# A state-space layer beside a feed-forward layer: the first tile's statistics, two weight pieces and a reciprocal block are reordered

## The chip, the cores and the metric

The kernel runs on one core of a Trainium2 chip. A core has a matrix engine (TensorE, in the profile PE, its weight loads PEld), a vector engine (VectorE, DVE), a scalar engine (ScalarE, ACT), GpSimd (POOL), and SyncE (SP), which here only issues transfers. Each engine runs its own list of instructions in order and waits on semaphores for the others. Transfers (DMA) are issued from the queues of SyncE, ScalarE and POOL. The metric is the time of one execution on the device, in microseconds.

## The reference: what is computed

The input `u` has 2048 rows of 576. A layer norm of it goes into two branches, and input and branches are added:

```python
x = A_u
xn = _layernorm(x, axis=-1)
return x + _A_ref(xn, A_A_re, ..., A_Dskip) + _B_ref(xn, B_w1, B_w2)
```

Branch B is a feed-forward layer, `silu(xn @ w1) @ w2` with 4608 hidden columns. Branch A is a state-space convolution: from nine small parameter arrays a kernel `K` of 2048 taps is made for each of the 576 channels, and each channel of `xn` is convolved with its `K` by a Fourier transform; `xn * Dskip` is added.

## The kernel before

**Matrix products in parts.** Every operand of a large product is split in a high part, rounded to the matrix engine's short format, and a low part, the rest. A product is then three: high by high, high by low, low by high. A name that ends in `h` is a high part, one that ends in `l` a low part: `xh`, `xl` of the normed input, `w1h`, `w1l` of the first weights, `w2h`, `w2l` of the second, `gh`, `gl` of the hidden values. A high part is a copy with rounding, on ScalarE; a low part is a subtraction, on VectorE.

**Tiles and blocks.** The 2048 rows are 16 tiles of 128 rows, loaded in pairs (`load_x`, lines 167 to 177; the first pair in eight transfers over the queues of SyncE and ScalarE). Four tiles make a block of 512 rows. `phase0` (line 210) treats tiles 0 to 7 at the start: `norm` (line 185) takes the statistics on VectorE (lines 192 and 193), adds a constant (196), has POOL raise the variance to the power -0.5 (197) and scales the tile (201, or 206 on ScalarE). `put_xt` (line 120) transposes a tile on TensorE into PSUM (124) and makes `xh` (125) and `xl` (126); `put_x4` (line 128) does the same with the last 64 columns of two tiles (132 to 134). `late` (line 897) treats tiles 8 to 15, whose transposed form goes through memory.

**The feed-forward part** (`ffn`, line 256) is the main program. The hidden columns come in nine chunks of four groups of 128, and all of it runs for two halves of the rows. For each half, chunk and block, `up` (line 316) makes a hidden group: twelve matmuls over the high and low parts and two for the last 64 columns (326 to 328), then SiLU and the split of the result (334 to 337). `down` (line 339) multiplies a tile's hidden values with the second weights (352) and adds the sum to an accumulator (356). The weights are loaded by `load_w1` (263) and `load_w2` (297) and split by `split_w1` (282) and `split_w2` (305). The first block's `up` works on its first two tiles, then on the other two, so that it can begin early.

**The state-space part** (`side`, line 858) is a second program beside it. It is a generator that stops at marks, fractions of the main program's length; `weave` (line 33) runs the main program step by step and lets the other go on when its mark is reached. `natural` (line 465) prepares the parameters on VectorE and ScalarE in five pieces; between its pieces lie the marks of the list in line 906. `gate_of(i)` (line 854) gives the marks that lie at the first step of a block.

**What sets the order.** The order in which the program states instructions is a priority, not the order of execution. A planner puts each engine's instructions in order before the run, by estimated times and these priorities; on the chip each engine then keeps that order. `behind(ins)` (line 141) forces what is stated inside it behind one instruction on that instruction's own engine. `pins` holds such instructions by name: `sdv` the addition of line 196, `xn` the scaling, `pt` the last transpose, `xt_h` the high part, `xt_v` the low part of the last 64 columns, `w1l` and `w2l` the weights' low parts. `idle(n)` (line 872) issues `n` matmuls of a zero tile that nothing reads; it is called with 12 at the very start, with 8 behind tile 0's transposes and with 3 behind tile 1's.

A transfer of the first weights comes in four pieces: rows 0 to 255, rows 256 to 511, and two of 64 KB for the last 64 rows, written to the two halves of the partitions.

Of the kernel before, what the change touches and what calls it, by code (L numbers as in the profile page):

```python
# [11 lines left out]
F32 = mybir.dt.float32  # L12
# [3 lines left out]
ALU = mybir.AluOpType  # L16
# [3 lines left out]
P = 128  # L20
L = 2048
D = 576
# [4 lines left out]
HD = D // 2  # L27
# [16 lines left out]
def kernel(  # L44
# [74 lines left out]

    def put_xt(xh, xl, src):  # L120

        pt = pss.tile([P, NKT, P], F32, tag="pss", name="pt")
        for kt in range(NKT):
            pins["pt"] = nc.tensor.transpose(pt[:, kt, :], src[:, kt * P:(kt + 1) * P], ident).ins
        pins["xt_h"] = nc.scalar.copy(xh, pt).ins  # L125
        nc.vector.tensor_sub(xl, pt, xh)  # L126

    def put_x4(x4, srcs):

        pt = pss.tile([P, 512], F32, tag="pss", name="pt4")  # L130
        for i, src in enumerate(srcs):
            pins["pt"] = nc.tensor.transpose(pt[:64, i * P:(i + 1) * P], src[:, NKT * P:D], ident).ins
        pins["xt_s"] = nc.scalar.copy(x4[:64, :], pt[:64, :2 * P]).ins
        pins["xt_v"] = nc.vector.tensor_sub(x4[64:, :], pt[:64, :2 * P], x4[:64, :]).ins

    xts = {}
    pairs = {}
    lasts = []
    pins = {}

# [38 lines left out]
    def store(t, j, engines):  # L179

        for hs in (slice(0, HD), slice(HD, D)) if j == NJ - 1 else (slice(0, D),):
            for ps, v, eng in quarters(ov, engines):
                eng.dma_start(v[:, j:j + 2] if len(t.shape) > 2 else v[:, j, hs], t[ps] if len(t.shape) > 2 else t[ps, hs])

    def norm(p0, js, xs):

# [23 lines left out]
    def phase0(p0, js, idle=None):  # L210

        xs = load_x(js[0], accp, "acc", (nc.sync, nc.scalar) if js[0] < 2 else (nc.sync,))
        acc.update(zip(js, xs))
        yield
        if js[0]:
            with behind(pins["w1l"] if js[0] == 2 else None):
                normed(p0, js, xs)
        else:
            for j, xj in zip(js, xs):
                with behind(pins["xn"] if j else None):  # L220
                    normed(p0, (j,), (xj,))
                if not j:
                    pins["xt0s"] = pins["xt_h"]
                with behind(pins["pt"]):
                    idle(3 if j else 8)
        pins[f"xt{js[1]}h"] = pins["xt_h"]
        pins[f"xt{js[1]}"], pins[f"xt{js[1]}s"] = pins["xt_v"], pins["xt_s"]
        yield

    def normed(p0, js, xs):  # L230
        xn = norm(p0, js, xs)
        for i, j in enumerate(js):
            b, jj = divmod(j, 4)
            if b < 2:
                if jj == 0:
                    xts[b] = new_xt(b)
                c = slice(jj * P, (jj + 1) * P)
                xh, xl, x4 = xts[b]
                put_xt(xh[:, :, c], xl[:, :, c], xn[:, i, :])
                lasts.append(xn[:, i, :])  # L240
                if jj % 2:
                    put_x4(x4[:, (jj - 1) * P:(jj + 1) * P], lasts)
                    lasts.clear()
# [12 lines left out]
    def ffn():  # L256
# [6 lines left out]
        def load_w1(half, c, t):  # L263
# [12 lines left out]
            else:  # L276
                nc.sync.dma_start(r1[:, 0:4, :], v1)
            nc.sync.dma_start(r1[0:64, 4, :], w1[512:576, fs])
            pins["load"] = eng.dma_start(r1[64:128, 4, :], w1[512:576, fs]).ins
# [59 lines left out]
        def down(blk, jj):  # L339
# [6 lines left out]
            for h in range(2):  # L346
# [8 lines left out]
                with tc.high_priority():  # L355
                    nc.vector.tensor_add(acc[j][:, hs], po[:, :HD], acc[j][:, hs])  # L356
            if half == 0 and c == NCH - 1:
# [107 lines left out]
    def natural(nat, par):  # L465
# [54 lines left out]
        v.tensor_scalar(t0, br, 1e-37, None, op0=ALU.max)  # L520
        for i in range(0, NT, 2):
            v.reciprocal(t0[:, i:i + 2], t0[:, i:i + 2])
        v.tensor_mul(t0, t0, bi)
# [9 lines left out]
        for i in range(0, 4 * D, D):  # L533
# [324 lines left out]
    def side():  # L858
# [3 lines left out]
        with tc.tile_pool(name="kf", bufs=1) as kfp:  # L862
            for n in ("f", "phi"):
                kf[n] = kfp.tile([P, D], F32, name=n + "T")
            with tc.tile_pool(name="par", bufs=1) as par:
                with tc.tile_pool(name="pa", bufs=4) as pa:
# [28 lines left out]
                with tc.tile_pool(name="nat", bufs=1) as nat, tc.tile_pool(name="pb", bufs=1) as pb:  # L895
                    nt = natural(nat, par)
                    def late(j):
# [3 lines left out]
                        with behind(pins["xn" if j == 8 else "gl"]):  # L901
                            normed(pb, (j, j + 1), xs)
                        yield

                    tiles = chain.from_iterable(late(j) for j in range(8, NJ, 2))
                    for at, todo in ((0.0, nt), (0.0, tiles), (0.004, tiles), (0.005, tiles), (gate_of(0), nt), (0.026, tiles), (0.028, tiles), (0.036, tiles), (0.038, tiles), (gate_of(1), nt), (0.06, tiles), (gate_of(2), nt), (0.09, nt)):
# [111 lines left out]
```

## Time and profile before

| | us |
|---|---|
| median of 3 runs | 1111.88 (1111.85 to 1111.98) |
| the profiled execution | 1111.65 |
| its span, first to last instruction | 1109.9 |
| TensorE busy | 1101.6 (99%) |
| VectorE busy | 916.1 (83%) |
| ScalarE busy | 707.3 (64%) |
| POOL busy | 71.0 (6%) |
| TensorE's last matmul ends | 1105.8 |
| granted TensorE clock, mean | 1.00 |

A row of a timeline has the start, the length, the engine, the line of the kernel, the operation, what it writes and reads (`out<-in`), the shapes and how many instructions were merged; in brackets stands how long the engine was idle before it and what released it. An engine's name with a `q` is its sequencer, which issues transfers. A row of waits has who waited for whom, the total in us, how often, and the longest. A row of transfers has how many, KB each and the median us from issue to landing. Lengths of matmuls overlap, since they are pipelined.

### The profile page before, as it was taken

How to read it: one execution, taken by the hardware profiler on the slowest of the kernel's cores; microseconds unless marked ns; L12 is line 12 of the kernel's file. 1: busy time of each engine (PE TensorE's matmuls, PEld its weight loads, DVE VectorE, ACT ScalarE, POOL GpSimd, SP SyncE). 2: the span in 40 equal slices, each digit the busy share in tenths (PEclk: the TensorE clock that was granted, in tenths of full speed). 3: DMA queues.
4: the chain of work that ended last, by engine and by line, in shares of the span. 5: the costliest groups of instructions: out<-in, count | busy, mean ns of one | idle time of the engine just before them, and what ended most of it. 6: DMA issues, size and time to landing. Idle time of an engine off the chain costs nothing.

```text
span 1109.9 us, 22912 instructions
## 1 busy us (share of the span) xinstructions
PE 1101.6 (99%) x9167; PEld 997.5 (90%) x9167; DVE 916.1 (83%) x1542; ACT 707.3 (64%) x1223; POOL 71.0 (6%) x127
## 2 busy tenths in 40 slices
PE   8999999999999999999999999999999999999998
PEld 6988999899889899899989989999999999999887
DVE  7799899999999999999999837787778778784433
ACT  4574466676677676677866536877777778774210
POOL 1100000000000000011000000000000000000111
PEclk9999999999999999999999999999999999999999
DMA  8745522425242525255734163554544445434973
GB/s 255 205 123 154 146 61 61 120 72 126 77 109 82 130 62 130 77 154 163 209 127 105 44 177 105 168 159 126 160 145 150 139 147 170 130 107 130 257 205 87
DMA packets 175851, 148.56 MB, mean 134 GB/s; under 512 B 111088, under 2 KB 142720, under 8 KB 175616
## 3 DMA queue, kind: packets, MB, share of 16 engines
q1 hardware_dynamic: 165408, 112.69, 37.8%
q0 software_dynamic: 9504, 33.49, 9.5%
q8 instruction: 72, 1.18, 0.5%
q10 hardware_dynamic: 832, 0.92, 0.3%
q14 instruction: 35, 0.29, 0.1%
HBM read 102.53 MB, written 44.61 MB: 133 GB/s over the span
## 4 chain that ended last, share of the span: by engine, by line
PE 97%; DMA 2%; SPq 0%; DVE 0%; ACT 0%; issue 0%; ACTq 0%
PE po L352 42%; PE ph L326 35%; PE kp L691 3%; PE ph L327 3%; PE ph L328 3%; PE pu L821 2%; PE pb L821 2%; PE pk L821 2%; PE z L706 2%; PE pu L160 1%; PE py L842 1%; PE pu L161 1%; DMA acc<-in_A_u_dram 1%; DMA w2r<-in_B_w_dram 1%; DMA w1r<-in_B_w_dram 0%; PE ptk L485 0%
## 5 line engine op out<-in xcount | busy, mean ns | idle before, releaser
L352 PE MATMUL po<-w2l,gh 128*128 128x288 f32 x1152 | 338.6, 296 | 1.2 <-DVE w2l L313 1.2
L352 PE MATMUL po<-w2h,gl 128*128 128x288 f32 x1152 | 336.6, 295 | 0.0
L352 PE MATMUL po<-w2h,gh 128*128 128x288 f32 x1152 | 336.4, 296 | 0.0
L352 PEld LDWEIGHTS po<-w2h,gh 128*128 128x128 f32 x1152 | 215.3, 188 | 7.6 <-issue 2.8
L352 PEld LDWEIGHTS po<-w2l,gh 128*128 128x128 f32 x1152 | 216.0, 188 | 6.5 <-DVE w2l L313 1.4
L352 PEld LDWEIGHTS po<-w2h,gl 128*128 128x128 f32 x1152 | 215.6, 188 | 0.9
L334 ACT ACTIVATE gf<-ph 128x512 f32<-128x512 f32 (+1 forms) x148 | 86.3, 584 | 145.3 <-PE ph L328 133.0
L326 PE MATMUL ph<-xh,w1h 128*128 128x512 f32 (+1 forms) x592 | 161.6, 387 | 0.3 <-ACT xh L125 0.3
L326 PE MATMUL ph<-xl,w1h 128*128 128x512 f32 (+1 forms) x592 | 161.5, 386 | 0.0
L326 PE MATMUL ph<-xh,w1l 128*128 128x512 f32 (+1 forms) x592 | 161.2, 385 | 0.0
L356 DVE TENSOR_TENSOR acc<-po,acc 128x288 f32<-128x288 f32 x288 | 126.9, 454 | 36.9 <-PE po L352 35.6
L337 DVE TENSOR_TENSOR gl<-gf,gh 128x512 fp32r<-128x512 f32 (+1 forms) x148 | 99.4, 675 | 64.5 <-ACT gh L335 63.7
L326 PEld LDWEIGHTS ph<-xh,w1l 128*128 128x128 f32 x592 | 108.1, 188 | 19.9
L326 PEld LDWEIGHTS ph<-xl,w1h 128*128 128x128 f32 x592 | 108.0, 188 | 20.0 <-DVE xl L126 0.2
L326 PEld LDWEIGHTS ph<-xh,w1h 128*128 128x128 f32 x592 | 104.6, 188 | 17.1 <-ACT xh L125 0.8
L335 ACT CAST gh<-gf 128x512 fp32r<-128x512 f32 (+1 forms) x148 | 89.6, 609 | 9.5 <-PE po L352 6.6
L648 ACT ACTIVATE c<-th,magic 128x1040 f32<-128x1040 f32 x36 | 42.1, 1169 | 37.7 <-DVE C L671 27.7
L650 ACT ACTIVATE c<-th 128x1040 f32<-128x1040 f32 x36 | 38.7, 1075 | 34.1 <-DVE th L649 34.1
L311 ACT CAST w2h<-w2r 128x576 fp32r<-128x576 f32 x72 | 47.0, 671 | 16.7 <-PE po L352 14.9
L292 DVE TENSOR_TENSOR w1l<-w1r,w1h 128x640 fp32r<-128x640 f32 x72 | 57.2, 823 | 0.2
L327 PE MATMUL ph<-x,w1h 128*128 128x512 f32 (+1 forms) x148 | 57.1, 386 | 0.0
L328 PE MATMUL ph<-x,w1l 128*128 128x512 f32 (+1 forms) x148 | 56.9, 385 | 0.0
(182 smaller groups left out, 1829.3 us busy)
## 6 DMA issues: line engine op xcount, KB each, us to landing
w2r<-in_B_w_dram SPq DMA_DIRECT2D x72, 288.0 KB, 3.7
w1r<-in_B_w_dram SPq DMA_DIRECT2D x35, 512.0 KB, 3.7
d1u<-u POOLq DMA_DIRECT2D x32, 288.0 KB, 2.5
d1k<-stage SPq DMA_DIRECT2D x18, 512.0 KB, 7.0
ur<-d1u SPq DMA_DIRECT2D x32, 288.0 KB, 3.4
kr<-d1k SPq DMA_DIRECT2D x32, 288.0 KB, 2.8
d<-yo POOLq DMA_DIRECT2D x32, 288.0 KB, 3.6
ys<-d SPq DMA_DIRECT2D x32, 288.0 KB, 10.7
```

The lines of the kernel that those rows point to most:

```text
L292: pins["w1l"] = nc.vector.tensor_sub(l1, src, h1).ins
L311: pins["w2h"] = nc.scalar.copy(h2, r2).ins
L326: nc.tensor.matmul(ph, w[:, kt, :], v[:, kt, a:e], start=n + kt == 0, stop=False)
L327: nc.tensor.matmul(ph, h1[:, 4, :], x4[:, a:e], start=False, stop=False)
L328: pins["pe"] = nc.tensor.matmul(ph, l1[:, 4, :], x4[:, a:e], start=False, stop=True).ins
L334: nc.scalar.activation(gf, ph, AF.Silu)
L335: pins["gh"] = nc.scalar.copy(gh, gf).ins
L337: pins["gl"] = nc.vector.tensor_sub(gl, gf, gh).ins
L352: pins["pe"] = nc.tensor.matmul(po[:, :HD], G[blk, t][g][:, js], W2[half, c, t][w][:, hs], start=n == 0, stop=n == 3 * FT - 1).ins
L356: nc.vector.tensor_add(acc[j][:, hs], po[:, :HD], acc[j][:, hs])
L648: nc.scalar.activation(c65, th, AF.Identity, bias=magic)
L821: nc.tensor.matmul(dst, st, mv[:, hs], start=n == 0, stop=n == 3 * len(terms) - 1)
```

## The change

Six things are moved; no arithmetic is added or taken away, apart from five filler matmuls that are dropped.

- **Tiles 0 and 1** go through a new function, `norm_apart`. Tile 0's statistics, its addition and its power on POOL are stated, then tile 1's statistics behind tile 0's addition, and only then both scalings, the first behind tile 1's addition.
- **`put_xt`** takes the engine of the high part as an argument, and returns the low part's subtraction in place of issuing it. For tile 1 the high part is made on VectorE, for all others on ScalarE as before. The low parts of two tiles are issued together, for tiles 0 and 1 behind tile 1's high part; the low part of the last 64 columns comes behind them.
- **Fillers** behind tile 0's transposes: 3 in place of 8.
- **Two 64 KB pieces** of the first weight transfer go to POOL's queue; one was on SyncE's, one on ScalarE's.
- **Statistics of tiles 4 and 5** stand behind the last `w2l` of the first chunk, as those of 6 and 7 did, in place of behind tile 3's last low part.
- **A block of `natural`** (three reciprocals and four passes after them) becomes a piece of its own, later: at a new mark three steps behind `gate_of(1)`, and behind the latest accumulator sum.

```diff
-    def put_xt(xh, xl, src):
+    def put_xt(xh, xl, src, copy):
...
-        pins["xt_h"] = nc.scalar.copy(xh, pt).ins
-        nc.vector.tensor_sub(xl, pt, xh)
+        pins["xt_h"] = copy(xh, pt).ins
+        return lambda: nc.vector.tensor_sub(xl, pt, xh).ins
...
-        pins["xt_v"] = nc.vector.tensor_sub(x4[64:, :], pt[:64, :2 * P], x4[:64, :]).ins
+        with behind(pins["xt_l"]):
+            pins["xt_v"] = nc.vector.tensor_sub(x4[64:, :], pt[:64, :2 * P], x4[:64, :]).ins
...
+    def norm_apart(p0, xs):
+
+        sds, mvs = [], []
+        for i in range(2):
+            st = p0.tile([P, 2, 6], F32, tag="st0", name="st0", bufs=2)
+            mv = p0.tile([P, 2], F32, tag="mv0", name="mv0", bufs=2)
+            sd = p0.tile([P, 1], F32, tag="sd0", name="sd0", bufs=2)
+            with behind(pins["sdv"] if i else None):
+                for h in range(2):
+                    nc.vector.bn_stats(out=st[:, h, :], in_=xs[i][:, h * HD:(h + 1) * HD])
+            nc.vector.bn_aggr(out=mv, in_=st)
+            pins["sdv"] = nc.vector.tensor_scalar(sd, mv[:, 1:2], 1e-5, None, op0=ALU.add).ins
+            pins["sd"] = nc.gpsimd.tensor_tensor(sd, sd, mhalf[:, :1], op=ALU.pow).ins
+            sds.append(sd)
+            mvs.append(mv)
+        for i in range(2):
+            xn = p0.tile([P, 1, D], F32, tag="xn0", name="xn0", bufs=2)
+            with behind(pins["xn"] if i else pins["sdv"]):
+                pins["xn"] = nc.vector.tensor_scalar(xn[:, 0, :], xs[i], mvs[i][:, 0:1], sds[i],
+                                                     op0=ALU.subtract, op1=ALU.mult).ins
+            yield xn
...
-            for j, xj in zip(js, xs):
-                with behind(pins["xn"] if j else None):
-                    normed(p0, (j,), (xj,))
+            for j, xn in zip(js, list(norm_apart(p0, xs))):
+                normed(p0, (j,), xn)
...
-                    idle(3 if j else 8)
+                    idle(3)
...
-                put_xt(xh[:, :, c], xl[:, :, c], xn[:, i, :])
+                low = put_xt(xh[:, :, c], xl[:, :, c], xn[:, i, :], nc.vector.tensor_copy if j == 1 else nc.scalar.copy)
+                lows.append(low)
                 lasts.append(xn[:, i, :])
+                if j:
+
+                    with behind(pins["xt_h"] if j == 1 else None):
+                        for low in lows:
+                            pins["xt_l"] = low()
+                    lows.clear()
...
-            nc.sync.dma_start(r1[0:64, 4, :], w1[512:576, fs])
+            if first and t == 0:
+                eng = nc.gpsimd
+            (eng if first and t == 0 else nc.sync).dma_start(r1[0:64, 4, :], w1[512:576, fs])
             pins["load"] = eng.dma_start(r1[64:128, 4, :], w1[512:576, fs]).ins
...
-                    nc.vector.tensor_add(acc[j][:, hs], po[:, :HD], acc[j][:, hs])
+                    pins["acc"] = nc.vector.tensor_add(acc[j][:, hs], po[:, :HD], acc[j][:, hs]).ins
...
-        for i in range(0, NT, 2):
-            v.reciprocal(t0[:, i:i + 2], t0[:, i:i + 2])
-        v.tensor_mul(t0, t0, bi)
-        v.tensor_scalar(t0, t0, 1.0, None, op0=ALU.min)
-
-        v.tensor_mul(t1, t0, t0)
-        v.tensor_scalar(t1, t1, 1.0, None, op0=ALU.add)
         yield
...
         nc.sync.dma_start(dexp, ex[:, :3 * D].rearrange("n (d k) -> n d k", k=3))
+        yield
+        for i in range(0, NT, 2):
+            v.reciprocal(t0[:, i:i + 2], t0[:, i:i + 2])
+        v.tensor_mul(t0, t0, bi)
+        v.tensor_scalar(t0, t0, 1.0, None, op0=ALU.min)
+
+        v.tensor_mul(t1, t0, t0)
+        v.tensor_scalar(t1, t1, 1.0, None, op0=ALU.add)
         yield
...
-                        with behind(pins["xt3" if js[0] == 4 else "w2l"]):
+                        with behind(pins["w2l"]):
...
-                    for at, todo in ((0.0, nt), (0.0, tiles), (0.004, tiles), (0.005, tiles), (gate_of(0), nt), ..., (gate_of(1), nt), (0.06, tiles), (gate_of(2), nt), (0.09, nt)):
+                    for at, todo in ((0.0, nt), (0.0, tiles), (0.004, tiles), (0.005, tiles), (gate_of(0), nt), ..., (gate_of(1), nt), (gate_of(1) + 3 / (4 * NCH * 2 * FT), nt), (0.06, tiles), (gate_of(2), nt), (0.09, nt)):
                         yield at
-                        with behind(pins["gl"] if at else pins["xt7"] if todo is nt else None):
+                        with behind(pins["acc" if todo is nt and at == gate_of(1) + 3 / (4 * NCH * 2 * FT) else "gl"] if at else pins["xt7"] if todo is nt else None):
                             next(todo, None)
```

More of the change, by code (lines that the diff above doesn't have):

```diff
@@ L138 @@
     lasts = []
+    lows = []
     pins = {}
@@ L216, in phase0 @@
             with behind(pins["w1l"] if js[0] == 2 else None):
-                normed(p0, js, xs)
+                normed(p0, js, norm(p0, js, xs))
         else:
-            for j, xj in zip(js, xs):
-                with behind(pins["xn"] if j else None):
-                    normed(p0, (j,), (xj,))
+            for j, xn in zip(js, list(norm_apart(p0, xs))):
+                normed(p0, (j,), xn)
                 if not j:
@@ L228, in phase0, with normed @@
         yield
-    def normed(p0, js, xs):
-        xn = norm(p0, js, xs)
+    def normed(p0, js, xn):
         for i, j in enumerate(js):
@@ L901, in late @@
                         with behind(pins["xn" if j == 8 else "gl"]):
-                            normed(pb, (j, j + 1), xs)
+                            normed(pb, (j, j + 1), norm(pb, (j, j + 1), xs))
                         yield
                     tiles = chain.from_iterable(late(j) for j in range(8, NJ, 2))
-                    for at, todo in ((0.0, nt), (0.0, tiles), (0.004, tiles), (0.005, tiles), (gate_of(0), nt), (0.026, tiles), (0.028, tiles), (0.036, tiles), (0.038, tiles), (gate_of(1), nt), (0.06, tiles), (gate_of(2), nt), (0.09, nt)):
+                    for at, todo in ((0.0, nt), (0.0, tiles), (0.004, tiles), (0.005, tiles), (gate_of(0), nt), (0.026, tiles), (0.028, tiles), (0.036, tiles), (0.038, tiles), (gate_of(1), nt), (gate_of(1) + 3 / (4 * NCH * 2 * FT), nt), (0.06, tiles), (gate_of(2), nt), (0.09, nt)):
                         yield at
-                        with behind(pins["gl"] if at else pins["xt7"] if todo is nt else None):
+                        with behind(pins["acc" if todo is nt and at == gate_of(1) + 3 / (4 * NCH * 2 * FT) else "gl"] if at else pins["xt7"] if todo is nt else None):
                             next(todo, None)
```

## The prediction

> **What bounds the kernel now.** I read the engine table first, then the waits of TensorE, then the timelines of TensorE and VectorE over the first 45 us, and the timelines of ScalarE, POOL and SyncE beside them. The engine table and the complete list of TensorE's waits:
>
> ```profile
> PE 1101.6 (99%) x9167; PEld 997.5 (90%) x9167; DVE 916.1 (83%) x1542; ACT 707.3 (64%) x1223; POOL 71.0 (6%) x127
> PE pz L874 <- DVE zero L869: 1.3, 1, 1.3
> PE pt L124 <- DVE xn L201: 1.2, 1, 1.2
> PE po L352 <- DVE w2l L313: 1.2, 1, 1.2
> PE ph L326 <- ACT xh L125: 0.3, 1, 0.3
> ```
>
> TensorE is busy 1101.6 of 1109.9 us and has four waits. The first is start-up, and 8.3 us of idle time is all there is: an edit can gain only by letting TensorE's real work begin earlier, or by taking a wait out of it. Where these waits lie on TensorE:
>
> ```profile
> 1.29 4.08 PE L874 MATMUL pz<-zero 128*128 128x512 bf16 x12 [1.29 <-DVE zero L869]
> 6.57 0.66 PE L124 MATMUL pt<-ident,xn 128*128 128x128 f32 x4 [1.21 <-DVE xn L201]
> 7.07 1.89 PE L874 MATMUL pz<-zero 128*128 128x512 bf16 x8
> 8.99 0.66 PE L124 MATMUL pt<-ident,xn 128*128 128x128 f32 x4
> ...
> 9.70 0.81 PE L874 MATMUL pz<-zero 128*128 128x512 bf16 x3
> 10.79 0.74 PE L326 MATMUL ph<-xh,w1h 128*128 128x256 f32 x4 [0.28 <-ACT xh L125]
> 11.52 0.74 PE L326 MATMUL ph<-xl,w1h 128*128 128x256 f32 x4
> ...
> 23.28 0.30 PE L352 MATMUL po<-w2h,gh 128*128 128x288 f32 x1
> 24.76 0.40 PE L352 MATMUL po<-w2l,gh 128*128 128x288 f32 x1 [1.18 <-DVE w2l L313]
> ```
>
> The rows of `zero` are fillers: they write nothing that is used and count as busy, so busy time before 10.79 is no work. The kernel's own matmuls start at 10.79 with the high parts and at 11.52 with the low parts of x; the one real stall lies at 23.28 to 24.76, on the first low part of the second weights. VectorE in the same stretch:
>
> ```profile
> 4.00 0.82 DVE L192 BATCH_NORM_STATS2 st<-acc 128x6 f32<-128x288 f32 x2 [2.76 <-DMA acc<-in_A_u_dram]
> ...
> 5.09 0.16 DVE L196 TENSOR_SCALAR sd<-mv 128x1 f32<-128x1 f32 x1
> ...
> 6.43 0.81 DVE L192 BATCH_NORM_STATS2 st<-acc 128x6 f32<-128x288 f32 x2
> ...
> 7.52 0.16 DVE L196 TENSOR_SCALAR sd<-mv 128x1 f32<-128x1 f32 x1
> 8.36 0.58 DVE L201 TENSOR_SCALAR xn<-acc,mv,sd 128x576 f32<-128x576 f32 x1 [0.68 <-POOL sd L197]
> ...
> 10.77 0.69 DVE L126 TENSOR_TENSOR xl<-pt,xh 128x512 fp32r<-128x512 f32 x1 [1.24 <-ACT xh L125]
> 11.49 0.42 DVE L134 TENSOR_TENSOR x<-pt,x 64x256 fp32r<-64x256 f32 x1
> 11.94 1.56 DVE L292 TENSOR_TENSOR w1l<-w1r,w1h 128x640 fp32r<-128x640 f32 x2
> 13.42 1.53 DVE L192 BATCH_NORM_STATS2 st<-acc 128x6 f32<-128x288 f32 x4
> ...
> 19.04 1.28 DVE L126 TENSOR_TENSOR xl<-pt,xh 128x512 fp32r<-128x512 f32 x2
> ...
> 22.51 1.54 DVE L192 BATCH_NORM_STATS2 st<-acc 128x6 f32<-128x288 f32 x4 [1.74 <-DMA acc<-in_A_u_dram]
> 23.96 2.08 DVE L313 TENSOR_TENSOR w2l<-w2r,w2h 128x576 fp32r<-128x576 f32 x3
> ```
>
> Here is the reason of the stall: VectorE stands idle 1.74 us for the load of tiles 4 and 5, takes their statistics (1.54 us), and only then makes w2l. The other engines, and how long a late x load takes to land (the last column of that row):
>
> ```profile
> 1.28 1.31 ACTq L175 DMA_DIRECT2D acc<-in_A_u_dram  x3
> ...
> 7.26 0.58 ACT L125 CAST xh<-pt 128x512 fp32r<-128x512 f32 x1 [4.56 <-PE pt L124]
> 9.53 0.72 ACT L290 CAST w1h<-w1r 128x640 fp32r<-128x640 f32 x1 [1.68 <-DMA w1r<-in_B_w_dram]
> 1.28 0.69 POOL L100 DMA_DIRECT2D ident<-in_cident_dram  x1 [0.83 <-POOLq L1005]
> 7.76 0.56 POOL L197 TENSOR_TENSOR sd<-sd,mhalf 128x1 f32<-128x1 f32 x1 [1.86 <-DVE sd L196]
> 15.48 1.31 POOL L197 TENSOR_TENSOR sd<-sd,mhalf 128x2 f32<-128x2 f32 x1 [7.16 <-DVE sd L196]
> 9.07 0.38 SPq L277 DMA_DIRECT2D w1r<-in_B_w_dram  x1
> acc<-in_A_u_dram ACTq DMA_DIRECT2D x2, 72.0 KB, 3.4
> ```
>
> **1. Statistics of tile 1 inside tile 0's power.** VectorE is free at 5.25 (5.09 + 0.16), but the last of the three loads that ScalarE's queue issues from 1.28 (0.44 each) leaves at about 2.15 and lands 3.4 later, about 5.5. So these statistics start near 5.55 in place of 6.43. From statistics to the end of the addition took 6.43 to 7.68, 1.25 us: 6.80. The scaling of tile 0 is put behind that addition, so it starts near 6.75, later than now, and its transposes, 0.63 after (8.36 to 8.99), at 7.4 and not 6.57. The power of tile 1 (0.56, 0.08 after the addition) ends at 7.45, its scaling at 8.05. Tile 0 pays 0.8 us, tile 1 gains about 0.9. The power may be held up: this one took 0.56 on one column, the one at 15.48 took 1.31 on two. If the power of tile 1 waits out the scaling of tile 0 (0.58), tile 1 is scaled at 8.6; the next step covers it.
>
> **2. Three fillers for eight.** They issue every 0.24 us or less (1.89 for 8), and stand between the two transposes. With tile 0's transposes at 7.4, three fillers begin at 7.9 (6.57 to 7.07 is 0.5) and the transposes of tile 1 at about 8.55: 0.44 before 8.99. Fillers that are taken away cost nothing themselves. What stands behind them, from transposes of tile 1 to the end of the last three, is 8.99 to 10.51, 1.5 us, so TensorE is free for real work at about 10.05.
>
> **3. High parts of tile 1 on VectorE, both low parts behind them.** The copy can start 0.69 after its transposes (6.57 to 7.26), 9.24. No row shows this copy; the nearest are ScalarE's cast of the same tile, 0.58, and VectorE's scaling of 576, 0.58, and a subtraction of 512 that takes 0.69 bounds it above. I take 0.58 and 0.54 from start to start: low part 0 at 9.78, low part 1 at 10.38 (two of them take 1.28, so 0.60 apart), ready at 11.06. Before, they were ready at 11.46. High parts are ready at 9.8. VectorE's own work grows by 0.58, in a gap of 1.24.
>
> **4. Two weight pieces on POOL's queue.** ScalarE's cast waits 1.68 us for these loads until 9.53. The two POOL issues, 0.69 each like ident's, come at 1.97 and 2.66, ahead of the power at 5.3. They are done by then, and take two issues from SyncE and ScalarE; SyncE's next loads come earlier (the second weights' load at 9.07 waited for the first one's landing). Whether the cast starts at 8.8 or still at 9.53, its end (9.5 to 10.25) lies before the low parts at 11.06 by more than four high-part matmuls take (0.6 us without a wait, estimated from 0.74 with one): worth nothing, costing nothing, unless the extra traffic pushes tile 1's load beyond 5.5. I allow 0.3 for that.
>
> Sum at the start: the low-part matmuls at 11.10 for 11.52, 0.4; VectorE's chain behind (x4 at 11.0 for 11.49, w1l at 11.45 for 11.94, statistics of tiles 2 and 3 at 12.9 for 13.42), 0.5. VectorE's chain is what TensorE follows from there, so I take **0.5 us**, between 0.1 (load late by 0.3, slow copy) and 0.95 (TensorE takes the second weight tile's high-part matmuls into the 0.5 us in which it waits for low parts).
>
> **5. Statistics of tiles 4 and 5 behind w2l.** VectorE is free at 20.77 (22.51 less 1.74), so at 20.3 with the shift; four w2l at 0.7 (2.08 for three) run until 23.1 if ScalarE's w2h come in time. TensorE asks for the first at about 23.5 less 0.5; it is ready at 21.0. The stall goes: 1.18 (the idle time) to 1.48 (start to start, which includes one regular step), I take **1.3**. What is late next: the statistics start at 23.1 and not 22.51. Their end users:
>
> ```profile
> 40.17 0.59 ACT L125 CAST xh<-pt 128x512 fp32r<-128x512 f32 x1
> 42.72 2.00 PE L326 MATMUL ph<-xh,w1h 128*128 128x512 f32 x8
> ```
>
> Tile 7's high part is ready at 40.76 and TensorE needs it at 42.72: 1.96 us to spare. TensorE comes 1.8 earlier, which leaves 0.16. The statistics' own delay is 0.6, but the w2l that stood between them and their scaling are gone from that place, so I count the chain as not later.
>
> **6. The reciprocal block later.** It moves, VectorE work only, behind the sixth sum of the second block, at 78.93:
>
> ```profile
> 67.67 4.96 DVE L522 RECIPROCAL t<-t 96x256 f32<-96x256 f32 x3
> 78.07 0.94 DVE L523 TENSOR_TENSOR t<-t,bi 96x768 f32<-96x768 f32 x1
> 78.93 0.45 DVE L356 TENSOR_TENSOR acc<-po,acc 128x288 f32<-128x288 f32 x1
> 60.00:130.00 70.00, 70.00 (x416) 63.43 (x415) 67.09 (x115) 36.57 (x48) 4.28 (x4) 1.00 0.55 148
> ```
>
> The last row (a stretch: length, then busy time and count of PE, PEld, DVE, ACT, POOL, clock, DMA) shows TensorE busy for all 70 us and VectorE for 67. Moving 4.96 plus four passes of at most 0.95, 8.8 us, cannot help a TensorE that never waits there; it can hurt if TensorE's transposes of its result come before the result. Cover: VectorE's 2.9 idle us. I count 0, with 2 us as the far end.
>
> **Sum.** 0.5 + 1.3 = 1.8 us off the profiled execution, 1111.65 (span 1109.9): 1109.85. The median of the runs is 0.23 above that execution, so the forecast is **1110.1**. 0.2%, 2.2 us, is about what can be told from no change; the forecast lies within it.
>
> **Rivals.**
> - *More at the start.* If TensorE fills the wait for low parts and VectorE's chain moves with it, 0.95 + 1.48 is 2.4 and the time 1109.4. For it: loads come earlier too. Against: VectorE's chain, with no gap from 10.77 to 15, sets the pace.
> - *A new wait for w2l's.* The order of each engine is planned ahead by estimated times; another operand (a gl, which queues on VectorE) may stop TensorE where w2l did. Then only the start's 0.5 is left: 1111.4. Against: VectorE's 1.74 idle us are filled and its queue is shorter.
> - *Tiles 4 to 7 late, ending slower than before.* The four w2l (2.8 us) go in front of the statistics and nothing behind gets shorter. Then tile 7 is ready at 43.55, TensorE asks at 40.9, waits 2.65, and the net is +0.85: 1112.7. It decides once the chain is more than 0.16 late, and loses all at 1.96. If VectorE delays it by another 1.4 us, it passes 1114.1. Against: w2l moves up by 3.6, and the idle 1.74 us pay for more than half of it.
> - *The clock.* The first twelve fillers took 0.34 each (4.08 for 12), the later eight 0.24, though the granted clock reads 1.00 throughout: TensorE starts slow and speeds up. Now it idles from 5.4 to 7.4, not 6.57, with five fillers fewer. If it falls back, some 3 us of matmuls take twice as long, 1.5 us, and the time is 1111.6. The Trainium skill, "TensorE: Matmul & The Clock Gate", section "What's actually happening", says that the array falls to half clock after at least one idle window of about 3.4 us; by that rule 2.0 us of idle keeps the clock and the sum stands. The trace agrees as far as it goes: after 1.21 idle us the later fillers ran fast.
>
> **How the numbers follow.** Forecast 0.57 (its own range 1109.3 to 1110.9), more at the start 0.15, new wait 0.12, late tiles 0.11, clock 0.05. Below 1109.66 lie most of the second case and a fifth of the first: 0.26. Above 1114.1 lies the late tiles' far end, alone or with the reciprocals' 2 us on top: 0.10. The range, 1109.0 to 1112.8, leaves out about one in ten on either side.
>
> **What would show it.** Tile 1's statistics at 5.5 and low parts at 11.1 at the start; no TensorE wait for w2l, and w2l done by 23.2; the 512-wide matmuls at about 40.9 without a wait; a reciprocal after 78 with TensorE's waits empty. A TensorE wait on xh, gl or a transposed t after 20 us, or slow fillers after 7 us, would make it wrong.

## The result, and the profile after

The changed kernel takes 1122.24 us, the kernel before 1111.87 (medians of six runs each): a ratio of 1.0094, 95% interval 1.0078 to 1.0111. It is slower by 10.4 us where the forecast had it faster by 1.8, and its time lies above the forecast's range (1109.0 to 1112.8).

The engine table, the first figures of the chain that ended last, and the longest of TensorE's waits in the kernel after (a row of waits: who waited for whom, us in total, how often, the longest):

```profile
PE 1105.1 (99%) x9162; PEld 997.6 (89%) x9162; DVE 917.0 (82%) x1543; ACT 707.9 (63%) x1223; POOL 75.2 (7%) x129
...
PE 59%; DVE 23%; issue 6%; DMA 5%; ACT 5%; SPq 1%; POOL 1%; ACTq 0%; DVEq 0%; POOLq 0%
...
PE po L384 <- ACT w2h L343: 2.6, 2, 1.7
PE po L384 <- DVE w2l L345: 2.0, 3, 0.8
PE py L875 <- DMA ys<-d: 1.9, 1, 1.9
PE pt L125 <- DVE xn L206: 1.6, 1, 1.6
PE pu L163 <- ACT stage L747: 1.6, 2, 0.8
```

Where the kernel before had four waits, of which only one came after 11 us, this one has five on the second weights alone, and others on the state-space part's `stage` and `ys`. In the chain that ended last, TensorE's own work is down to 59%; before it was:

```profile
PE 97%; DMA 2%; SPq 0%; DVE 0%; ACT 0%; issue 0%; ACTq 0%
```

The start of the kernel after, from the timelines of PE, DVE, ACT and POOL:

```profile
8.20 0.66 PE L125 MATMUL pt<-ident,xn 128*128 128x128 f32 x4 [1.61 <-DVE xn L206]
8.69 0.81 PE L907 MATMUL pz<-zero 128*128 128x512 bf16 x3
10.81 1.18 PE L358 MATMUL ph<-xh,w1h 128*128 128x256 f32 x8
11.92 1.21 PE L358 MATMUL ph<-xl,w1h 128*128 128x256 f32 x8
23.52 0.30 PE L384 MATMUL po<-w2l,gh 128*128 128x288 f32 x1
41.49 2.00 PE L358 MATMUL ph<-xh,w1h 128*128 128x512 f32 x8
...
6.40 0.82 DVE L197 BATCH_NORM_STATS2 st<-acc 128x6 f32<-128x288 f32 x2 [1.04 <-DMA acc<-in_A_u_dram]
8.60 0.58 DVE L206 TENSOR_SCALAR xn<-acc,mv,sd 128x576 f32<-128x576 f32 x1 [0.45 <-POOL sd L200]
9.97 0.69 DVE L126 CAST xh<-pt 128x512 fp32r<-128x512 f32 x1 [0.80 <-PE pt L125]
10.58 1.28 DVE L127 TENSOR_TENSOR xl<-pt,xh 128x512 fp32r<-128x512 f32 x2
21.05 2.76 DVE L345 TENSOR_TENSOR w2l<-w2r,w2h 128x576 fp32r<-128x576 f32 x4
75.16 4.96 DVE L568 RECIPROCAL t<-t 96x256 f32<-96x256 f32 x3
...
7.73 0.83 POOL L200 TENSOR_TENSOR sd<-sd,mhalf 128x1 f32<-128x1 f32 x1 [1.72 <-DVE sd L199]
```

The second weights' low part is asked for at 23.52 with no wait, so the stall that the change is to remove has gone, and the wide matmuls at 41.49 have none either. The first real matmul starts at 10.81, as before. Up to here the kernel after is 1.2 us ahead.

To see where the rest went I compared the two traces at equal work: for each moment of one, how many columns TensorE has done so far without the fillers, and when the other has done as many. This is my own calculation from the starts of the matmuls, and good to some tenths. After minus before, in us, at times of the kernel before:

| at | 20 | 30 | 100 | 130 | 250 | 262 | 386 | 450 | 510 | 566 | 1030 | end |
|---|---|---|---|---|---|---|---|---|---|---|---|---|
| after | +0.2 | -1.2 | -1.1 | +0.2 | -1.1 | +1.5 | +3.1 | +3.7 | +6.3 | +9.5 | +9.2 | +11.2 |

The loss comes in steps, nearly all of it hundreds of microseconds behind any edit. TensorE's largest waits there are for `w2l` (at 258, 384 and 447 us of the kernel after), `w2h` (507 and 569), `stage` (512 and 574) and `ys` (1043). All its waits behind 11 us add up to 8.6 us, before to 1.2, so the waits on record hold 7.4 of the 11.2; the rest stands as busy time and is not explained here. One row each, from the costliest groups, shows what is new over the whole run: ScalarE's rounding of the second weights, first before, then after (behind the bar: busy time, mean ns of one, then how long ScalarE was idle just before these casts and what ended most of it):

```profile
L311 ACT CAST w2h<-w2r 128x576 fp32r<-128x576 f32 x72 | 47.0, 671 | 16.7 <-PE po L352 14.9 <-DMA w2r<-in_B_w_dram 1.7
```

```profile
L343 ACT CAST w2h<-w2r 128x576 fp32r<-128x576 f32 x72 | 46.7, 672 | 41.7 <-DMA w2r<-in_B_w_dram 21.7 <-PE po L384 19.8
```

The casts are the same 72 and take the same time, but ScalarE waits 21.7 us for the loads of the second weights and not 1.7. At one of the larger steps, 500 to 512 us, the timelines of SyncE, ScalarE and TensorE after read as follows; the last row is a piece of the chain that ended last, the load's time from issue to landing:

```profile
497.71 0.33 SPq L153 DMA_DIRECT2D xr<-dxn  x1
498.50 1.00 SPq L334 DMA_DIRECT2D w2r<-in_B_w_dram  x2
...
507.39 0.67 ACT L343 CAST w2h<-w2r 128x576 fp32r<-128x576 f32 x1 [5.38 <-DMA w2r<-in_B_w_dram]
...
508.12 0.40 PE L384 MATMUL po<-w2h,gh 128*128 128x288 f32 x1 [0.83 <-ACT w2h L343]
512.43 0.41 PE L163 MATMUL pu<-sp,s 128*128 128x288 f32 x1 [0.75 <-ACT stage L747]
...
498.50 8.87 DMA w2r<-in_B_w_dram
```

and SyncE before:

```profile
487.20 0.33 SPq L150 DMA_DIRECT2D xr<-dxn  x1
493.38 4.99 SPq L302 DMA_DIRECT2D w2r<-in_B_w_dram  x3
```

By their count these are the same loads, and TensorE itself is 3.8 us behind here. The load of the state-space part's `xr` leaves 10.5 us later than before, close ahead of the weights, which leave 5.1 later; and the first of these takes 8.87 us to land, amid other transfers, so that it lands 11 us later than before, 7 more than TensorE's own delay. Behind it ScalarE waits 5.38 us, and what is queued on ScalarE behind that cast (`stage`) stops TensorE once more.

### The profile page after: what moved, and what is told of

Same layout as the page of the kernel before. It is cut to its first block, busy times and chain, and to the rows that moved or that the text cites. A ratio compares the mean times of both kernels' runs of the same rounds, so it can differ in the third digit from the quotient of the medians.

```text
span 1121.2 us, 22902 instructions
## 1 busy us (share of the span) xinstructions
PE 1105.1 (99%) x9162; PEld 997.6 (89%) x9162; DVE 917.0 (82%) x1543; ACT 707.9 (63%) x1223; POOL 75.2 (7%) x129
## 3 DMA queue, kind: packets, MB, share of 16 engines
q8 instruction: 72, 1.18, 0.4%
## 4 chain that ended last, share of the span: by engine, by line
PE 59%; DVE 23%; issue 6%; DMA 5%; ACT 5%; SPq 1%; POOL 1%; ACTq 0%; DVEq 0%; POOLq 0%
PE po L384 25%; PE ph L358 20%; DVE acc L388 3%; PE pu L854 2%; PE pk L854 2%; PE pb L854 2%; DVE gl L369 2%; DMA w2r<-in_B_w_dram 2%; DVE C L692 2%; PE ph L359 2%; PE ph L360 2%; DVE S L703 2%; DVE th L665 2%; DVE th L682 1%; DVE w1l L324 1%
## 5 line engine op out<-in xcount | busy, mean ns | idle before, releaser
L343 ACT CAST w2h<-w2r 128x576 fp32r<-128x576 f32 x72 | 46.7, 672 | 41.7 <-DMA w2r<-in_B_w_dram 21.7
L345 DVE TENSOR_TENSOR w2l<-w2r,w2h 128x576 fp32r<-128x576 f32 x72 | 53.2, 752 | 8.4 <-ACT w2h L343 8.2
## 6 DMA issues: line engine op xcount, KB each, us to landing
ys<-d SPq DMA_DIRECT2D x32, 288.0 KB, 11.2
```

What stands on the lines that cost most here:

```text
L343: pins["w2h"] = nc.scalar.copy(h2, r2).ins
L345: pins["w2l"] = nc.vector.tensor_sub(l2, r2, h2).ins
```

## The experiments

Two theories, with the letters that the expectations use. **A**: one of the moved parts makes something late at its place, and its cost stays with it. **B**: any of them changes the estimated times from which the planner orders the later work, and the new order, 60 to 600 us on, makes the loss. The letters C and D stand for what the expectations say beside them. To tell the theories apart I also compared the order that is planned for VectorE with that of the kernel before: the share of instructions that stand in the same sequence in both lists. This is a count of the lists and no view of the profile.

**The start alone.** The changed kernel with the two other parts undone:

```diff
-                        with behind(pins["w2l"]):
+                        with behind(pins["xt3" if js[0] == 4 else "w2l"]):
```

and the reciprocal block back in its old place.

> The kernel before with the start's edits alone (tile 1's statistics in the wait, three fillers, high part on VectorE, two weight pieces on POOL's queue). Theory A, the moved reciprocal block is what costs: no loss here, 1111.5 to 1112.2, since the changed kernel's low-part matmuls begin no earlier than before. Theory B, any shift of the planned times makes the planner lay out the middle of the kernel anew and some layouts stop TensorE: a loss of 2 us or more, not related to the part, 1113 to 1121. Theory C, the w2l edit costs: 1111.5 to 1112.2.

Measured: 1111.85 us (10 runs), before 1112.22; ratio 0.9997 (0.9987 to 1.0006). The list agrees to 99.9%. Neither gain nor loss: the start is not what costs the ten microseconds, and it does not bring its half microsecond. The loss of 2 us or more that theory B forecast for any shift did not come, and neither did a new order.

**The statistics of tiles 4 and 5 alone**, in the kernel before:

```diff
-                        with behind(pins["xt3" if js[0] == 4 else "w2l"]):
+                        with behind(pins["w2l"]):
```

> The kernel before with the statistics of tiles 4 and 5 behind w2l alone. Theory A: the stall of 1.4 us goes and nothing else changes, 1110.4 to 1110.8. Theory B: the stall goes, but waits of 2 us or more appear between 100 and 600 us, 1112 to 1120. Theory C: nearly the whole loss, 1119 to 1123.

Measured: 1119.85 us (4 runs); ratio 1.0076 (1.0055 to 1.0097). The w2l wait is gone, and at equal work this kernel is 1.8 us ahead from 25 to 60 us; then come new waits, the longest of them:

```profile
PE po L352 <- ACT w2h L311: 2.0, 1, 2.0
PE po L352 <- DVE acc L356: 2.0, 2, 1.8
```

The list agrees to 45% only. What an order of this kind does is seen at 430 to 446 us, where the edit has long been done and TensorE is 3.0 us behind at equal work. TensorE, ScalarE and SyncE before:

```profile
441.01 0.29 PE L352 MATMUL po<-w2h,gl 128*128 128x288 f32 x1
...
443.26 0.43 PE L352 MATMUL po<-w2h,gh 128*128 128x288 f32 x2
...
441.78 0.66 ACT L311 CAST w2h<-w2r 128x576 fp32r<-128x576 f32 x1
...
438.83 1.00 SPq L302 DMA_DIRECT2D w2r<-in_B_w_dram  x2
```

and with this edit:

```profile
443.88 0.30 PE L352 MATMUL po<-w2h,gl 128*128 128x288 f32 x1
446.19 0.52 PE L352 MATMUL po<-w2h,gh 128*128 128x288 f32 x2 [2.01 <-ACT w2h L311]
...
446.98 0.44 PE L352 MATMUL po<-w2l,gh 128*128 128x288 f32 x1
...
445.46 0.67 ACT L311 CAST w2h<-w2r 128x576 fp32r<-128x576 f32 x1 [3.07 <-DMA w2r<-in_B_w_dram]
...
442.10 1.00 SPq L302 DMA_DIRECT2D w2r<-in_B_w_dram  x2
```

The weight loads leave 3.3 us later and the cast of the new `w2h` comes 3.7 us later, little more than the 3.0 by which everything is late. What is new is TensorE's own order. Before, sixteen other products of 2.1 us together stood between its two rows, and the cast was done in that time; with this edit the new `w2h` is asked for right behind the first row, and TensorE waits 2.0 us for it. Behind the wait a product takes 0.44 us and not 0.29: the granted clock is 0.50 from 446.9 to 450.3 us, which costs about 1.7 us more (an estimate, half of 3.4). At equal work the kernel goes from 2.9 us behind at 440 to 6.8 at 450.

**The reciprocal block alone**, in the kernel before: the second half of `natural`'s third piece becomes a piece of its own, with its mark and behind the accumulator's sum, as in the change.

```diff
-        for i in range(0, NT, 2):
-            v.reciprocal(t0[:, i:i + 2], t0[:, i:i + 2])
...
         nc.sync.dma_start(dexp, ex[:, :3 * D].rearrange("n (d k) -> n d k", k=3))
+        yield
+        for i in range(0, NT, 2):
+            v.reciprocal(t0[:, i:i + 2], t0[:, i:i + 2])
```

> The kernel before with the reciprocal block moved alone. Theory A: nearly the whole loss, 1119 to 1123, with the first 100 us as before. Theory B: some loss, 1113 to 1120, of another layout than in the changed kernel. Theory C: no loss, 1111.5 to 1112.2.

Measured: 1118.68 us (7 runs); ratio 1.0064 (1.0043 to 1.0086); the list agrees to 65%. The largest wait of this kernel ends at 101 us; TensorE, ScalarE in front of it, and TensorE's next row:

```profile
101.04 1.19 PE L326 MATMUL ph<-xh,w1h 128*128 128x512 f32 x4 [2.79 <-ACT gf L334]
...
92.28 1.28 ACT L545 ACT_TABLE_LOAD   x1
...
94.83 1.35 ACT L290 CAST w1h<-w1r 128x640 fp32r<-128x640 f32 x2
96.20 1.28 ACT L547 ACT_TABLE_LOAD   x1
...
99.09 1.28 ACT L334 ACT_TABLE_LOAD   x1
100.39 1.09 ACT L334 ACTIVATE gf<-ph 128x512 f32<-128x512 f32 x2
...
102.07 1.81 PE L326 MATMUL ph<-xl,w1h 128*128 128x512 f32 x4
```

The block feeds a chain of table loads and activations on ScalarE. It began at 86.69 us in the kernel before and begins at 92.28 here, two weight casts (1.35 us) stand inside it, and the two SiLUs that TensorE waits for come behind the last table load. The row behind the wait takes 1.81 us where four such matmuls took 1.07 at 95.82: the granted clock is 0.50 from 102.2 to 105.6 us. In part this is theory A: the work that is moved does delay what stands behind it. At equal work this kernel goes from 1.5 us ahead at 98 to 3.2 behind at 104, 4.7 us, of which the wait is 2.8 and the clock about 1.7. The end of the profiled execution is 5.6 behind, so this one place holds most of the loss. In the full change, whose order differs again, TensorE has no wait at this place: the same two SiLUs come as late (at 100.65), but another one stands ahead of the second table load.

**One filler less**, eight to seven behind tile 0's transposes, in the kernel before: about 0.24 us less delay and nothing else.

```diff
-                    idle(3 if j else 8)
+                    idle(3 if j else 7)
```

> The kernel before with seven fillers in place of eight behind tile 0's transposes, and nothing else: no real work is changed or moved. Theories A and C: 1111.6 to 1112.1, within 0.3 us of before. Theory B: the planned times shift by up to 0.2 us, and if the layout of the middle is that sensitive the time moves by 1 us or more, either way.

Measured: 1112.10 us (10 runs); ratio 0.9997 (0.9988 to 1.0006). The list agrees to 100%. With the first experiment this narrows theory B: not any shift costs, only one that changes the order.

**The statistics of tiles 4 and 5, with four fillers more behind tile 1's transposes**, a number with which the order stays (99%):

```diff
-                    idle(3 if j else 8)
+                    idle(7 if j else 8)
...
-                        with behind(pins["xt3" if js[0] == 4 else "w2l"]):
+                        with behind(pins["w2l"]):
```

> The statistics of tiles 4 and 5 behind w2l, as in the run with that edit alone, and seven fillers in place of three behind tile 1's transposes. The four fillers delay the planned start so much that the planner's order of VectorE, ScalarE and SyncE beyond 65 us is that of before again (VectorE's lists agree to 99%, in place of 45% without the fillers). Theory B, the layout of the middle is what costs: the stall of 1.4 us goes, the fillers cost 0.2 to 0.6, and the time is 0.8 to 1.2 us below before. Theory D, the edit itself does harm later, through tiles 4 to 7: 4 us or more above before, as without the fillers.

Measured: 1110.46 us (11 runs), before 1111.53; ratio 0.9992 (0.9984 to 1.0001). The same edit that cost 7.6 us (1119.85 against 1112.22) now costs nothing; a gain of 1 us is likely and not clear of the noise. Its only wait behind the start:

```profile
PE po L352 <- ACT w2h L311: 0.8, 1, 0.8
```

**Only a delay**, nine fillers for three behind tile 1's transposes in the kernel before; no work that is used is touched:

```diff
-                    idle(3 if j else 8)
+                    idle(9 if j else 8)
```

> The kernel before with nine fillers in place of three behind tile 1's transposes, nothing else: a delay of TensorE by 0.9 us, with no real work moved by hand. The planner lays out the middle anew (VectorE's list agrees to 50% with before). Theory B: 3 to 9 us above before, with waits of TensorE on w2h, w2l, gf or sums at 60 to 120 and 370 to 580 us. Theory D: 0.9 us above before.

Measured: 1121.23 us (6 runs); ratio 1.0095 (1.0076 to 1.0114): the whole loss of the change. The list agrees to 50%. Its waits for `w2h`, and ScalarE at the place that was shown above:

```profile
PE po L352 <- ACT w2h L311: 2.6, 2, 2.0
...
447.37 0.67 ACT L311 CAST w2h<-w2r 128x576 fp32r<-128x576 f32 x1 [3.16 <-DMA w2r<-in_B_w_dram]
```

At equal work it is 1.1 us ahead at 60 us (its w2l wait is gone too) and 8.9 behind at the end. The delay is 0.7 us of fillers (2.11 for 1.46 with six), so the delay itself is not what costs. The loss is just above the 3 to 9 us of theory B's forecast.

**The start without the pieces on POOL's queue**: as the first experiment, and

```diff
-            if first and t == 0:
-                eng = nc.gpsimd
-            (eng if first and t == 0 else nc.sync).dma_start(r1[0:64, 4, :], w1[512:576, fs])
+            nc.sync.dma_start(r1[0:64, 4, :], w1[512:576, fs])
```

> The start's edits with the two weight pieces left on the queues of SyncE and ScalarE; the layout of the middle is that of before. If the pieces on POOL's queue were what made tile 1's load late (it landed at 6.28 in the changed kernel, 5.50 before), tile 1's statistics start near 5.55 here, low-part matmuls near 11.1 and the time is 0.3 to 0.8 us below before. If the start's edits are worth nothing for another reason, the time is within 0.2 us of before.

Measured: 1111.16 us (11 runs); ratio 0.9999 (0.9990 to 1.0007). At equal work it is 0.5 us ahead at 15 us, and level at 25: in the profiled execution the gain is there and is swallowed by the wait for `w2l`. In the time of the runs it is not clear of the noise.

```profile
5.82 0.82 DVE L197 BATCH_NORM_STATS2 st<-acc 128x6 f32<-128x288 f32 x2 [0.50 <-DMA acc<-in_A_u_dram]
...
PE po L382 <- DVE w2l L343: 1.5, 1, 1.5
```

**The start and the statistics of tiles 4 and 5**, without the reciprocal block's move (the changed kernel with that block back in its old place):

> The changed kernel with the reciprocal block back in its old place. Theory A as first stated (the reciprocals alone cost) has fallen already, since the w2l edit alone cost 7.6 us. Theory B: the layout is that of the w2l edit alone to a few places, so the loss is the same, 5 to 9 us above before. If the losses of the two parts added up, 7.6 here and 6.5 for the reciprocals would make 14, and the changed kernel's 10.4 is less than that.

Measured: 1127.75 us (5 runs); ratio 1.0144 (1.0123 to 1.0165). This is slower than the full change by 5.5 us, with one part less, slower than the two parts' own times would give (-0.4 and +7.6), and beyond the 5 to 9 us that theory B forecast. VectorE's list agrees to 45% with before and to more than 99% with that of the second experiment, but the waits in it are longer, the first on the state-space part:

```profile
PE z L738 <- ACT kt L730: 3.6, 1, 3.6
PE po L384 <- DVE acc L388: 3.4, 3, 2.7
...
1050.70:1057.40 6.70, 6.19 (x49) 4.93 (x50) 4.00 (x8) 0.90 (x2) 1.13 (x3) 0.50 1.07 234
```

The last row is a stretch, as in the prediction; its granted clock is 0.50. There are three such stretches in this profile, 13.7 us together, each behind a wait of 2.7 us or more (2.7, 3.6 and 2.7). By estimate they cost up to 6.8 of the 20.2 us by which this execution, the slowest of the five, ends behind. The change has no wait that long and no such stretch in its profile, so a good part of the difference between these two profiles is the clock.

**The same two parts, the order kept**: without the POOL pieces (which by the first experiment and the one without them make no difference to the time), and with ten fillers for three behind tile 1's transposes, with which the list agrees to 98.7%:

```diff
-                    idle(3)
+                    idle(10 if j else 3)
```

> The changed kernel without the move of the reciprocal block and without the two weight pieces on POOL's queue (both pieces back on the queues of before), with ten fillers for three behind tile 1's transposes, a number chosen so that VectorE's planned list agrees with that of the kernel before in 98.7% of its places. Theory B (the planned order makes the loss): the w2l stall is gone and no new wait comes, 1110.0 to 1111.0 us, ratio 0.9985 to 0.9995, against 1127.75 of the same two parts with three fillers. Theory A (the moved work itself costs; statistics of tiles 4 and 5 behind w2l together with the new start make later work late): 1116 us or more, with waits of TensorE after 60 us.

Measured: 1110.60 us (11 runs), before 1112.02; ratio 0.9992 (0.9983 to 1.0001). In this profile `w1h` makes TensorE wait 0.4 and `w2h` 0.2, and nothing else does after 8 us. Its profiled execution ends 0.2 us before that of the kernel before.

**Six fillers**, the twin of the nine:

```diff
-                    idle(3 if j else 8)
+                    idle(6 if j else 8)
```

> The kernel before with six fillers for three behind tile 1's transposes: a delay and nothing else, with the planned order unchanged (100% of VectorE's list). Twin of the run with nine fillers, whose order changed in half of its places and which took 1121.2 us. Theory B: no new wait after 25 us, 1111.5 to 1112.5 us, ratio 0.9995 to 1.0008; the w2l stall may be shorter, since TensorE's first real matmuls come up to 0.7 us later. Theory A' (a delay at the start as such makes the loss, in proportion to it): half of the loss with nine fillers, 1116 us.

Measured: 1111.82 us (12 runs, 1110.22 to 1115.5); ratio 1.0003 (0.9995 to 1.0012); the list agrees to 100%. The profiled execution is the slowest of the twelve. At equal work it is 3.0 us behind at 30 us and still 3.0 at 1030: what it loses up to there, it loses at the start. About 0.6 of it are the fillers, 1.0 a longer wait for `w2l` (2.15 for 1.18), and the rest the granted clock, 0.50 from 26.8 to 30.2 us, behind that wait.

All together, each ratio against the kernel before in the same series (1111.53 to 1112.22 us), with ScalarE's idle time ahead of the `w2h` casts that a `w2r` load ended (the row shown above, of each profile; two more of these rows stand below the table):

| kernel | order kept | us | ratio | `w2h` waits for `w2r` |
|---|---|---|---|---|
| six fillers | 100% | 1111.82 | 1.0003 | 2.3 |
| one filler less | 100% | 1112.10 | 0.9997 | 1.9 |
| start alone | 99.9% | 1111.85 | 0.9997 | 3.5 |
| start without POOL pieces | 99.9% | 1111.16 | 0.9999 | 1.9 |
| tiles 4 and 5, four fillers more | 99% | 1110.46 | 0.9992 | 4.1 |
| start, tiles 4 and 5, ten fillers | 98.7% | 1110.60 | 0.9992 | 3.0 |
| reciprocals alone | 65% | 1118.68 | 1.0064 | 11.2 |
| the change | 51% | 1122.24 | 1.0094 | 21.7 |
| nine fillers | 50% | 1121.23 | 1.0095 | 14.5 |
| tiles 4 and 5 alone | 45% | 1119.85 | 1.0076 | 17.2 |
| start, tiles 4 and 5 | 45% | 1127.75 | 1.0144 | 23.4 |

Tiles 4 and 5 alone, and nine fillers:

```profile
L311 ACT CAST w2h<-w2r 128x576 fp32r<-128x576 f32 x72 | 46.9, 672 | 36.5 <-PE po L352 19.2 <-DMA w2r<-in_B_w_dram 17.2
```

```profile
L311 ACT CAST w2h<-w2r 128x576 fp32r<-128x576 f32 x72 | 47.1, 672 | 33.4 <-PE po L352 18.7 <-DMA w2r<-in_B_w_dram 14.5
```

Nothing lies between: with the order kept all six ratios are within 0.1% of 1, whatever was edited (the moved reciprocal block is not among them); with another order all five are slower by 6 to 16 us, even if only fillers were added. Theory B holds, except perhaps for the reciprocals' 4.7 us at 101 us, which theory A claims with as much right.

What stays open: why each of the new orders loses its own amount. The waits name the second weights' loads and casts; at 507 us of the change the load lands late, at 446 us of the second experiment TensorE's own order asks for the weights earlier. Which of the thousands of changed places matters, the runs do not separate. The full change, with the reciprocal block, was not run with the order kept. Nor was a third buffer for `w2r` tried, which would let these loads leave earlier.

## Why the prediction was wrong, step by step

- **1, tile 1's statistics at 5.55.** They began at 6.40, since the load came late, and the power of tile 1 took 0.83 and not 0.56. Its scaling began at 8.60 and ended at 9.18, past the step's fallback too ("tile 1 is scaled at 8.6", an end: 8.05 and 0.58). Without the POOL pieces the statistics began at 5.82.
- **2, the fillers.** Three fillers took 0.81, near enough to the step's 0.24 each. The transposes came later than it had them, with the load: tile 0's at 8.20 for 7.4, tile 1's at 9.34 for 8.55.
- **3, VectorE's copy.** 0.69, the bound that the step named, and not the 0.58 that it took. The low parts were ready at 11.86 (10.58 + 1.28) and not 11.06.
- **4, the pieces on POOL's queue.** "Worth nothing, costing nothing" was wrong. The step allowed 0.3 for the delay of tile 1's load; the statistics came 0.85 late (6.40 against 5.55), 0.27 of which is there without the pieces too. That took away the start's gain: the matmuls on low parts began at 11.92, 0.4 later than before, though TensorE filled the wait with high-part work, as the first rival had it.
- **5, the w2l stall.** It went: from 20 to 30 us the kernel after gains 1.4 at equal work. `w2l` was done by 23.8 for the predicted 23.2, early enough for TensorE. Tile 7's part held too: the wide matmuls at 41.49 did not wait. The rival of late tiles is refuted. The stall's price, 1.3, was read from one execution: two other profiles of the same order (one filler less, six fillers) have it at 2.0 and 2.1 us, and the clock halved for 3.4 us behind it.
- **6, the reciprocal block.** Its far end of 2 us was too low: alone it costs 6.5 us (1118.68 against 1112.22), and in its profile 4.7 are lost at its place, 2.8 of them by the wait and the rest by the clock. The reciprocals came at 75.16, not after 78. The step looked for its cost in VectorE's cover and in "TensorE's transposes of its result"; what it hit in the run of its own is ScalarE, where the chain behind it now stands in front of two SiLUs.
- **The sum.** This is the step that failed. It adds the edits' own times on a timeline that is otherwise that of before, and so puts the cost of a new order at nothing. The prediction itself says that the order of each engine is planned by estimated times, and uses this for one rival only, the wait that would take the place of the w2l stall; there it prices it at the 1.3 us that would not be gained. It had to be priced over the rest of the run: from 30 to 1030 us the kernel after loses 10.4 us at equal work, and nine fillers alone, which change the order as much, cost 9.7 (1121.23 against 1111.53). VectorE busy for 67 of 70 us and a TensorE that never waits, which the prediction read as cover, come from an order in which the parts happen to fit; three fillers more (nine against six, 0.7 us) are enough to replace that order.
- **The clock.** At the start of the change it did not fall: after 1.61 idle us the next three fillers took 0.81, as the last three before. But the rival's mechanism and its 1.5 us are real. In the start alone TensorE was idle 2.70 us at the same place, the granted clock was 0.50 from 7.9 to 11.3 us, and the three fillers took 1.49. The prediction looked for it at the start only; the long waits of a new order bring it later in the run.

Where the order was kept, the sum points the right way, as far as can be told: the start (without the POOL pieces) and w2l, forecast to give 1.8 us, took 1110.60 against 1112.02. The interval (0.9983 to 1.0001) reaches 1, and the profiled executions end 0.2 us apart, so this does not show the gain.

## What to carry to other kernels

Where a planner orders the instructions by estimated times, an edit has two prices: its own, which can be read from the timeline, and that of the new order of all that follows, which cannot. Compare the planned lists before trusting a sum; if they differ, price the new order by a bare delay (some fillers), which shows how much a reshuffle alone is worth, and try to hold the order with such a delay before judging the edit. And look at the loads that have little room: here, in every slow order, ScalarE waited 11 to 23 us for the second weights (two buffers, one queue), and 2 to 4 in the others. That this is the cause and not a companion of the loss is not shown. A wait of TensorE of 2 us or more can cost more than itself, since the clock may be halved behind it.

## What was not expected of the hardware

- With two pieces of 64 KB on POOL's queue, a load came later that ScalarE's queue had issued at its usual time, 2.14 us: tile 1's last part landed at 6.28 to 6.43 us in the three profiles with the pieces and at 5.39 to 5.80 in the nine without. The loads of the next two tiles also leave earlier with them (3.68 to 3.77 us for 4.71 to 5.18), since SyncE has one issue less in front; the runs do not separate the two. The Trainium skill, "Trainium Kernel Development and Optimization", section "Key Constraints", says that the queues of SyncE, ScalarE and POOL run on the same transfer engines and interleave, so that issuing from several saves only issue time; the trace agrees in that a load of one queue came later for those of others.
- POOL's power of one column took 0.83 us beside VectorE's scaling of tile 0 (0.56 in the kernel before). The Trainium skill, "SBUF — State Buffer", section "SBUF: two separate sides", names a port pair of the on-chip memory that VectorE and POOL share under an exclusive lock, which certain VectorE instructions take; the 0.27 us more fit with this, but no run here separates the cause.
- VectorE's copy with rounding out of PSUM took 0.69 us, as long as a subtraction of the same shape.
- A wait of TensorE of little more than 2 us can halve its clock. In the twelve profiles all five waits of 2.69 us and more were followed by 3.4 us (once 6.8) at a granted clock of 0.50, three of the five from 2.01 to 2.33 us were, and none up to 1.89. One such stretch costs about 1.7 us (an estimate, half of 3.4). The rule that the prediction quotes from the Trainium skill, "TensorE: Matmul & The Clock Gate", section "What's actually happening", needs about 3.4 us of idle time. It does not hold here as it stands: shorter waits were enough.
- The clock is also a part of the spread of a kernel's runs. The seven runs of the reciprocals alone: 1115.25 us at a mean clock of 1.000, 1117.29 to 1118.68 at 0.998, 1120.61 and 1120.69 at 0.996, 1124.72 at 0.993.
